# One round of weight conversion moves from unit 15 to unit 4, and four subtractions before the last layer move from VectorE to GpSimd

## The chip, the cores and the metric

The kernel runs on one core of a Trainium2 chip. The metric is the device time of one execution in microseconds; less is better. The engines are named as the profile names them: PE is TensorE's matmul, PEld its weight load, DVE is VectorE, ACT is ScalarE, POOL is GpSimd, SP is SyncE, which issues the DMAs here.

## The reference, cut to what matters

Windowed attention feeds a mixture of four experts, weighted per token, and that feeds an MLP with a gate. The MLP's weights arrive as float64.

```python
x = attention(q, k, v)                       # 1152 tokens x 512
p = domain_probs / (domain_probs.sum(-1, keepdims=True) + 1e-09)
out = np.zeros((N, D), dtype=np.float32)
for e in range(4):
    h = np.maximum(x @ w1[e], 0.0)           # 512 -> 1024
    out += p[:, e:e + 1] * (h @ w2[e])       # 1024 -> 512
h = out @ w_in                               # 512 -> 2048, w_in and w_out are float64
g = h * (1.0 / (1.0 + np.exp(-1.702 * h)))
return (g @ w_out).astype(np.float32)
```

## The kernel before, in words

Every fp32 matmul is done as three matmuls on an upper and a lower part of each operand: high x high, high x low, low x high. The upper part is a rounding copy made by ACT, the lower part a subtraction made by DVE or POOL.

After the attention and the first expert (up to 136.91 us) the work goes by **units** of 256 hidden columns. Units 4 to 15 are the experts 1 to 3 (the mixture); units 16 to 23 are the MLP. Tokens are split in two halves: c = 0 has 512 tokens as 2 x 256 columns, c = 1 has 640 as 2 x 320. The first layer of a unit and half, named ("1", s, c), is done by `first2` as seven block products instead of eight, into four PSUM banks in the order a, c, b, d, a, c, d. Each product is six matmuls (L798); the fourth product d uses the weight sums `wsh`/`wsl`, the last product adds to bank d again. Between the two uses of bank d, DVE must read it (`s`, L817, which is s + d). So the last product of a pass waits for that L817. The second layer of a unit and half is ("2", s, c), with accumulation by L912.

The order on PE is ("1", s, 0), ("2", s-1, 1), ("1", s, 1), ("2", s, 0) for each unit. After each product or output tile a **slot** is run: side work that is issued there by hand-written tables, `FIRST` for unit 4, `MID` for units 5 to 14, `TURN` from unit 15 to 18. A table's fields, divided by "|", are the slots in order. In a field, `p.s.i` are the steps of `w1_prep` for unit s (weight sums on POOL at L677, upper parts on ACT, lower parts `wal` L681 and `wsl` L685 on POOL unless `BY_VECTOR` names them), `q.s.i` those of `w2_prep` (`w2l`, L696), `l` weight loads, `d` a step of the gate or the shares that had been put off, and `c.c.m.i` the steps of `x2_turn`, which makes for the MLP the differences `xt` (L622) and the upper and lower parts of the mixture's output.

The side work of interest is the **conversion of float64 words to fp32**, 32 rounds in all. A round is taken up step by step by the letter `w`: a load of one round's words two rounds ahead, a (two ACT passes, L730 and L731, on the loaded tile `sd`), b (DVE, L736, reads `sd` and makes `m`), c (DVE, L740, and then POOL, L741, both on `m`), and the store of the round before. The tile `sd` has three buffers and `m` two. `x.0` and `x.1` are the first two loads.

Every engine runs its instructions in the order in which they are issued, so an instruction that waits holds up all behind it on its engine. SP's queue does the same for DMAs.

Of the kernel before, what the change touches and what calls it, by code (L numbers as in the profile page):

```python
# [13 lines left out]
ALU = mybir.AluOpType  # L14
# [95 lines left out]
def fused_kernel(ctx: ExitStack, tc: tile.TileContext, qk, v, dp, w1, w2, w_in, w_out, out):  # L110
# [17 lines left out]
    nc = tc.nc  # L128
# [457 lines left out]
    S0 = SM - 1  # L586
    HOLD = ((4, 1), (15, 0), (18, 0),)
    LOWER = {(0, 0): "ppp", (0, 1): "pvp", (1, 0): "pvv", (1, 1): "vvp"}
    TILES = (range(0, 4), range(4, 9))
    queue = []  # L590
    turn_ = [0]
# [11 lines left out]
    def combos(c, m, xf, t, whole, lo_engines=(nc.vector,) * 3):  # L603

        n, t0, q0 = N_[c], T0[c], Q0[c]
        th, tl = (late["t"][:, y, :, m, q0:q0 + n] for y in range(2))
        b = xf
        fns = []

        def lo_(eng, out_, whole_, hi_):  # L610
            eng.tensor_tensor(out=out_, in0=whole_, in1=hi_.bitcast(F32), op=ALU.subtract)

        def block(y, l):
            kt = 2 * (y // 2) + m
            cols = slice(t0 + l * n, t0 + (l + 1) * n)
            return [lambda: nc.scalar.activation(xh[:, kt, cols], b[y], AF.Copy),
                    lambda: lo_(nc.vector if c == 0 or y == 3 else lo_engines[0], xl[:, kt, cols], b[y], xh[:, kt, cols])]

        if whole:
            fns += block(0, 0)  # L620
        for y, (p, q_) in enumerate(((b[1], b[0]), (b[3], t[:, 0]), (b[3], b[1]), (b[2], t[:, 1]))):
            fns.append(lambda y=y, p=p, q_=q_: nc.vector.tensor_tensor(out=t[:, y], in0=p, in1=q_, op=ALU.subtract))  # L622
        for x, ys in enumerate((slice(0, 2), slice(2, 4))):
            fns.append(lambda ys=ys: nc.scalar.activation(th[:, ys, :], t[:, ys], AF.Copy))
            fns.append(lambda x=x, ys=ys: lo_(lo_engines[1 + x], tl[:, ys, :], t[:, ys], th[:, ys, :]))
        if whole:
            fns += block(2, 0) + block(3, 1)
        return fns
# [4 lines left out]
    def x1_combos(c, m, it):  # L633

        n, t0 = N_[c], T0[c]
        made = []

        def join():
            xf, t = big_pair(c, f"1_{c}{m}")
            for j in range(2):  # L640
                parts_ = [x.bitcast(F32)[:, 2 * j + m, t0:t0 + 2 * n].rearrange("p (l n) -> p l n", l=2) for x in (xh, xl)]
                nc.gpsimd.tensor_tensor(out=xf[:, 2 * j:2 * j + 2], in0=parts_[0], in1=parts_[1], op=ALU.add)
            made.extend(combos(c, m, [xf[:, y] for y in range(4)], t, False))

        def some(a_, b_):
            for fn in made[a_:b_]:
                fn()
        at_it(it, join)
        at_it(it + 1, lambda: some(0, 4))
        at_it(it + 2, lambda: some(4, 8))  # L650

    def x2_turn(c, m):

        n, t0 = N_[c], T0[c]
        pool = f"big{c}"
        t = late[pool].tile([P, 4, n], F32, tag=pool, name=f"xt2_{c}{m}")
        b = [final[c, h, 2 * j + m] for j in range(2) for h in range(2)]
        return combos(c, m, b, t, True, [{"p": nc.gpsimd, "v": nc.vector}[x] for x in LOWER[c, m]])


    BY_VECTOR = ("p.15.2", "p.15.3", "p.15.9", "p.16.0", "p.17.1", "p.17.2", "p.18.3", "p.18.5", "p.18.7", "q.16.1", "q.16.3", "q.17.3", "u.16.1", "u.17.1",)
    ENDS = {(15, 0): 1, (15, 1): 0, (17, 0): 0}

    def engine(name):
        return nc.vector if name in BY_VECTOR else nc.gpsimd

# [252 lines left out]
    def second2(s, c, slots):  # L919
        n = N_[c]  # L920
        h = hbuf2[s, c]
        wh, wl = wt[s, 1]
        for i, t in enumerate(TILES[c]):

            end = s == SE - 1 and c == 1 and i == len(TILES[c]) - 1
            for cols in (slice(0, DM // 2), slice(DM // 2, DM)) if end else (slice(0, DM),):
# [84 lines left out]
    def order_of(keys):  # L1011
        pe = [("1", keys[0])]
        for x in range(1, len(keys)):
# [10 lines left out]
    pe += order_of([(SM, 1), (SM + 1, 1)] + [(s, c) for s in range(SM + 2, SE) for c in range(2)])[1:]  # L1024

    TURN = {
# [18 lines left out]
    }  # L1045

    FIRST = {
# [3 lines left out]
    }  # L1051

    MID = {
# [49 lines left out]
    def due(kind, s, c):  # L1103

        one = 7 + len(TILES[1 - c])
        if kind == "1":
# [86 lines left out]
```

## Time and profile before

| what | value |
|---|---|
| median of 3 runs | 618.14 us (617.94 to 618.57) |
| profiled execution | 618.13 us |
| its span, first to last instruction | 616.4 us |
| PE busy in the span | 609.0 us (99%) |
| DVE, POOL, ACT busy | 477.1, 360.1, 273.0 us |
| granted TensorE clock | 1.00 throughout |

The profiled execution's 618.13 us is its span and 1.73 us around it. It lies 0.01 us from the median of the runs. A busy PE is not a PE at its peak, since the ends of matmuls are modelled: short waits are read from the distance of starts.

### The profile page before, as it was taken

The numbers are of one execution on the slowest core, as the hardware profiler recorded it, in microseconds if no ns is written. First come the engines' busy times: TensorE is split into PE (matmuls) and PEld (weight loads), VectorE is DVE, ScalarE is ACT, GpSimd is POOL, SyncE is SP. The second block draws the span as 40 slices with busy tenths as digits, with TensorE's granted clock in tenths as the row PEclk, the third lists the DMA queues.
The fourth block names the chain that finished last, engine by engine and source line by source line (L and its number), as shares of the span: only waits on it lengthen the run. The fifth ranks groups of instructions, "written<-read, shape, count | busy, mean of one in ns | idle before, by whom it ended". The sixth has DMA issues, their size and how long they took to land.

```text
span 616.4 us, 11216 instructions
## 1 busy us (share of the span) xinstructions
PE 609.0 (99%) x4153; PEld 569.9 (92%) x4153; DVE 477.1 (77%) x1006; ACT 273.0 (44%) x603; POOL 360.1 (58%) x340
## 2 busy tenths in 40 slices
PE   7999999999999999999999999999999999999997
PEld 5999999999999999999999999899898988998996
DVE  6987623968888888888888899999977667667565
ACT  7965111344434444444354453446555444444321
POOL 6564003675777877868669765767509473473310
PEclk9999999999999999999999999999999999999999
DMA  8874246013544555535456435022103121100004
GB/s 316 286 245 122 81 119 216 1 34 137 172 126 149 151 179 155 149 127 166 123 152 184 147 104 171 35 87 71 65 2 103 35 70 35 34 1 1 0 2 154
DMA packets 30502, 69.44 MB, mean 113 GB/s; under 512 B 6732, under 2 KB 11248, under 8 KB 30448
## 3 DMA queue, kind: packets, MB, share of 16 engines
q1 hardware_dynamic: 30448, 68.73, 35.4%
q8 instruction: 32, 0.52, 0.4%
q14 instruction: 22, 0.18, 0.1%
HBM read 55.99 MB, written 12.73 MB: 111 GB/s over the span
## 4 chain that ended last, share of the span: by engine, by line
PE 94%; DVE 3%; issue 1%; ACT 1%; POOL 1%; POOLq 0%; DVEq 0%; ACTq 0%
PE gd L798 10%; PE gc L798 10%; PE ga L798 9%; PE g L532 8%; PE q L902 8%; PE q L904 8%; PE q L903 8%; PE q L932 5%; PE q L930 5%; PE q L931 5%; PE gb L798 5%; PE pa L566 3%; PE pa L568 3%; PE pa L567 3%; DVE xt L622 0%
## 5 line engine op out<-in xcount | busy, mean ns | idle before, releaser
L902 PE MATMUL q<-h,w2h 128*128 128x320 f32 (+1 forms) x288 | 97.4, 338 | 0.1
L904 PE MATMUL q<-h,w2h 128*128 128x320 f32 (+1 forms) x288 | 97.2, 337 | 0.0
L903 PE MATMUL q<-h,w2l 128*128 128x320 f32 (+1 forms) x288 | 97.2, 337 | 0.0
L845 DVE TENSOR_TENSOR h<-cc,h 128x256 fp32r<-128x256 f32 (+1 forms) x80 | 73.9, 924 | 20.0 <-ACT h L835 12.5
L741 POOL TENSOR_TENSOR m<-m,sd 128x512 int32<-128x512 int32 x32 | 49.1, 1534 | 62.8 <-ACT h L835 36.8
L685 POOL TENSOR_TENSOR wsl<-ss,wsh 128x512 fp32r<-128x512 f32 x39 | 59.6, 1535 | 31.0 <-ACT wsh L684 20.6
L835 ACT ACTIVATE h<-cc 128x256 fp32r<-128x256 f32 (+3 forms) x48 | 32.9, 686 | 99.1 <-DVE cc L832 98.8
L912 DVE TENSOR_TENSOR acc<-q,acc 128x512 f32<-128x512 f32 (+1 forms) x132 | 69.9, 546 | 8.3 <-PE q L904 7.1
L820 POOL TENSOR_TENSOR cc<-s,u 128x256 f32<-128x256 f32 (+1 forms) x38 | 33.4, 878 | 59.9 <-DVE s L817 59.9
L904 PEld LDWEIGHTS q<-h,w2h 128*128 128x128 f32 x288 | 54.1, 188 | 4.4
L902 PEld LDWEIGHTS q<-h,w2h 128*128 128x128 f32 x288 | 54.1, 188 | 4.2 <-DVE acc L912 0.3
L903 PEld LDWEIGHTS q<-h,w2l 128*128 128x128 f32 x288 | 54.1, 188 | 3.9
L932 PE MATMUL q<-w2h,h 128*128 128x512 f32 (+1 forms) x146 | 56.9, 390 | 0.0
L930 PE MATMUL q<-w2h,h 128*128 128x512 f32 (+1 forms) x146 | 56.7, 389 | 0.0
L931 PE MATMUL q<-w2l,h 128*128 128x512 f32 (+1 forms) x146 | 56.5, 387 | 0.0
L696 POOL TENSOR_TENSOR w2l<-st,w2h 128x512 fp32r<-128x512 f32 x37 | 53.0, 1444 | 5.5 <-ACT w2h L695 5.2
L939 DVE SCALAR_TENSOR_TENSOR acc<-q,acc 128x512 f32<-128x512 f32 (+1 forms) x64 | 42.6, 677 | 11.7 <-PE q L932 11.3
L681 POOL TENSOR_TENSOR wal<-st,wah 128x512 fp32r<-128x512 f32 (+1 forms) x38 | 48.0, 1268 | 2.3 <-ACT wah L680 2.3
L798 PE MATMUL ga<-xh,wal 128*128 128x256 f32 (+1 forms) x160 | 47.3, 296 | 0.0
L798 PE MATMUL ga<-xl,wah 128*128 128x256 f32 (+1 forms) x160 | 47.3, 295 | 0.0
L798 PE MATMUL ga<-xh,wah 128*128 128x256 f32 (+1 forms) x160 | 47.2, 295 | 0.0
L832 DVE SCALAR_TENSOR_TENSOR cc<-cc,pb 128x256 f32<-128x256 f32 (+3 forms) x48 | 41.8, 871 | 1.0
(368 smaller groups left out, 1730.2 us busy)
## 6 DMA issues: line engine op xcount, KB each, us to landing
st<-in_w_dram SPq DMA_DIRECT2D x32, 512.0 KB, 5.0
sd<-in_w_in_dram SPq DMA_DIRECT2D x16, 512.0 KB, 4.1
sd<-in_w_out_dram SPq DMA_DIRECT2D x16, 512.0 KB, 4.0
w<-m SPq DMA_DIRECT2D x32, 256.0 KB, 4.4
st<-w SPq DMA_DIRECT2D x16, 512.0 KB, 3.5
out_dram<-acc SPq DMA_DIRECT2D x8, 256.0 KB, 2.0
pb<-pd SPq DMA_DIRECT2D x3, 320.0 KB, 3.5
pb<-pd SPq DMA_DIRECT2D x3, 256.0 KB, 4.5
```

The costliest lines, as they stand in the source:

```text
L532: nc.tensor.matmul(pt[:, :C], w[:, kt, fs], xx[:, kt, c * C:(c + 1) * C], start=first and y == 0, stop=not todo and y == len(products[x]) - 1)
L685: fns.append(lambda x=x, dst=dst: engine(f"p.{s}.{x}").tensor_tensor(out=sl[:, dst], in0=sums[:, dst], in1=sh[:, dst].bitcast(F32), op=ALU ...
L696: fns.append(lambda o=o: engine(f"q.{s}.{2 * o + 1}").tensor_tensor(out=lo[:, o], in0=t[:, o], in1=hi[:, o].bitcast(F32), op=ALU.subtract))
L798: nc.tensor.matmul(bank_[:, :n], wz[:, y, m, :], xz, start=start and m == 0 and z == 0, stop=m == 1 and z == 2, skip_group_check=not start)
L845: nc.vector.tensor_tensor(out=hl[:, sub], in0=cc[:, sub], in1=hh[:, sub].bitcast(F32), op=ALU.subtract)
L902: nc.tensor.matmul(pt, wh[:, o, cols], hi, start=first, stop=False, skip_group_check=both)
L903: nc.tensor.matmul(pt, wl[:, o, cols], hi, start=False, stop=False, skip_group_check=both)
L904: nc.tensor.matmul(pt, wh[:, o, cols], lo, start=False, stop=last, skip_group_check=both)
L912: nc.vector.tensor_tensor(out=dst[:, on], in0=pt[:, on], in1=src[:, on], op=ALU.add)
L930: nc.tensor.matmul(pt, hi, wh[:, o, cols], start=o == 0, stop=False)
L931: nc.tensor.matmul(pt, hi, wl[:, o, cols], start=False, stop=False)
L932: nc.tensor.matmul(pt, lo, wh[:, o, cols], start=False, stop=o == 1)
```

## The change

One round's worth of conversion steps leaves the slots of ("1", 15, 0), where five `w` stood, and joins unit 4, where nine `w` stand instead of four; the first two loads move forward. From then on every round comes one round earlier in its table than before, up to the end. At the turn from mixture to MLP, three differences (`xt`, 128x320) go from DVE to POOL, and so does one lower part (`w2l` of unit 17, 128x512); one ACT copy and what follows it moves by a slot.

```diff
+    BY_POOL = ((1, 0, 3), (1, 1, 0), (1, 1, 3))
...
-            fns.append(lambda y=y, p=p, q_=q_: nc.vector.tensor_tensor(out=t[:, y], in0=p, in1=q_, op=ALU.subtract))
+            eng = nc.gpsimd if whole and (c, m, y) in BY_POOL else nc.vector
+            fns.append(lambda y=y, p=p, q_=q_, eng=eng: eng.tensor_tensor(out=t[:, y], in0=p, in1=q_, op=ALU.subtract))
...
-    BY_VECTOR = (..., "q.16.1", "q.16.3", "q.17.3", "u.16.1", "u.17.1",)
+    BY_VECTOR = (..., "q.16.1", "q.16.3", "u.16.1", "u.17.1",)
...
-        ("1", 15, 0): " |  | w | w | w | w w | ",
+        ("1", 15, 0): " |  |  |  |  |  | ",
...
-        ("1", 16, 0): "q.17.1 c.1.0.12 | q.17.2 c.1.0.4 c.1.0.3 |  | c.1.0.10 c.1.0.5 | c.1.0.0 c.1.0.6 |  | q.16.3 c."
+        ("1", 16, 0): "q.17.1 c.1.0.12 | q.17.2 c.1.0.4 c.1.0.3 |  | c.1.0.10 | c.1.0.5 c.1.0.0 c.1.0.6 |  | q.16.3 c."
...
     FIRST = {
-        ("1", 0): "q.0 p.6 p.0 p.2 p.1 |  |  | p.3 q.2 l.0 |  | x.0 | p.4 | x.1",
-        ("1", 1): "p.8 d | p.7 q.1 | d w p.9 | w | d | p.10 w |  | p.5",
-        ("2", 0): "d |  |  | p.11 l.1 d w d q.3",
+        ("1", 0): "q.0 p.6 p.0 p.2 p.1 | x.0 |  | p.3 q.2 l.0 | x.1 |  | p.4 | ",
+        ("1", 1): "p.8 d w | p.7 q.1 | d w p.9 | w | d w | p.10 w | w | p.5 w",
+        ("2", 0): "d | w |  | p.11 l.1 d w d q.3",
```

In what follows rows of the changed kernel have line numbers that are 1 or 2 higher. A row is the line, the operation, output <- inputs with a running number, and the shape; the brackets say whose semaphores it waits on.

**DVE in ("1", 4, 1) and after it.** Before, from the sum u of that pass on:

```order
L815 TENSOR_TENSOR u_4_1_2056<-gb_1_2052,s_4_1_2054 128x320 [waits PE_49,Activation_49]
L817 TENSOR_TENSOR s_4_1_2057<-gd_1_2053,s_4_1_2055 128x320 [waits PE_49,Activation_49]
L845 TENSOR_TENSOR h_0_2026<-cc_0_1974,h_0_2026 128x768 [waits Activation_49]
L832 SCALAR_TENSOR_TENSOR cc_1_2058<-ga_1_2050,pb_1512_1952 128x320 [waits DMAHW2_49,PE_49]
L845 TENSOR_TENSOR h_1_2105<-cc_1_2058,h_1_2105 128x320 [waits Activation_49]
L736 TENSOR_SCALAR m_2116<-sd_2036 128x512 [waits DMAHW4_49]
```

With the change (its step b of round 0 is the row of m_2096, its step c the next one of m_2096):

```order
L817 TENSOR_TENSOR u_4_1_2056<-gb_1_2052,s_4_1_2054 128x320 [waits PE_49,Activation_49]
L738 TENSOR_SCALAR m_2096<-sd_2000 128x512 [waits DMAHW3_49,Activation_49]
L819 TENSOR_TENSOR s_4_1_2057<-gd_1_2053,s_4_1_2055 128x320 [waits PE_49]
L847 TENSOR_TENSOR h_0_2030<-cc_0_1974,h_0_2030 128x768 [waits DVE_49]
L742 SCALAR_TENSOR_TENSOR m_2096<-sd_2000,m_2096 128x512 [waits DVE_49]
L834 SCALAR_TENSOR_TENSOR cc_1_2058<-ga_1_2050,pb_1512_1952 128x320 [waits DMAHW2_49,PE_49]
L847 TENSOR_TENSOR h_1_2109<-cc_1_2058,h_1_2109 128x320 [waits Activation_49]
```

Step b of round 0 has moved up by four rows, in front of s, and it waits there for ACT; step c follows three rows later. Round 1 is new in unit 4: its step b stands ahead of the first L912 of ("2", 4, 0), its step c behind the second.

**POOL at the end of unit 4.** Before, from the sum cc of ("1", 4, 1) on; `wsl_1988` is the lower part of unit 5's weight sums:

```order
L820 TENSOR_TENSOR cc_1_2058<-s_4_1_2057,u_4_1_2056 128x320 [waits DVE_49]
L681 TENSOR_TENSOR wal_1986<-st_5_1603,wah_1985 128x512
L685 TENSOR_TENSOR wsl_1988<-ss_1984,wsh_1987 128x512 [waits Activation_49,Pool_49]
L741 TENSOR_TENSOR m_2116<-m_2116,sd_2036 128x512 [waits DMAHW0_49,DMAHW4_49,DVE_49,PE_49]
L696 TENSOR_TENSOR w2l_1982<-st_5_1605,w2h_1981 128x512
```

With the change:

```order
L822 TENSOR_TENSOR cc_1_2058<-s_4_1_2057,u_4_1_2056 128x320 [waits DVE_49]
L743 TENSOR_TENSOR m_2096<-m_2096,sd_2000 128x512 [waits DMAHW0_49,DVE_49,DMAHW3_49,PE_49,Activation_49]
L683 TENSOR_TENSOR wal_1986<-st_5_1603,wah_1985 128x512
L743 TENSOR_TENSOR m_2134<-m_2134,sd_2028 128x512 [waits DMAHW5_49,DVE_49,Activation_49]
L687 TENSOR_TENSOR wsl_1988<-ss_1984,wsh_1987 128x512 [waits Pool_49]
L698 TENSOR_TENSOR w2l_1982<-st_5_1605,w2h_1981 128x512
```

Two conversion steps now stand ahead of `wsl_1988`, and the second is step c of round 1.

**DVE at the turn, in ("1", 16, 0) and ("1", 17, 0).** With the change, from s of unit 16 to s of unit 17:

```order
L819 TENSOR_TENSOR s_16_0_5381<-gd_0_5377,s_16_0_5379 128x256 [waits PE_49,Activation_49]
L843 SCALAR_TENSOR_TENSOR cc_0_5382<-th_0_5428,ga_0_5374 128x256 [waits Activation_49]
L855 TENSOR_TENSOR cc_0_5382<-gc_0_5375,u_16_0_5380 128x256 [waits DVE_49,PE_49]
L847 TENSOR_TENSOR h_0_5427<-cc_0_5382,h_0_5427 128x256 [waits Activation_49]
L698 TENSOR_TENSOR w2l_5308<-st_16_4830,w2h_5307 128x512
L861 TENSOR_TENSOR cc_0_5382<-gd_0_5377,u_16_0_5380 128x256 [waits PE_49]
L612 TENSOR_TENSOR t<-xt_10_5364,t 128x2x320 [waits Activation_49]
L843 SCALAR_TENSOR_TENSOR cc_0_5382<-th_0_5428,cc_0_5382 128x768 [waits Activation_49]
L817 TENSOR_TENSOR u_17_0_5456<-gb_0_5452,s_17_0_5454 128x256 [waits PE_49,Activation_49]
L819 TENSOR_TENSOR s_17_0_5457<-gd_0_5453,s_17_0_5455 128x256 [waits PE_49,Activation_49]
```

Before, an `xt` stood ahead of the first row, a `w2l` behind the L612 row and an `xt` behind the second L843 row. These three now stand on POOL, between its sums cc of unit 16 and of unit 17; the fourth moved operation comes after the sum of unit 17.

## Rows read from the trace of the kernel before

**Rows 1.** The page: head, busy time of each engine, a DMA issue (last: us to landing).

```profile
span 616.4 us, 11216 instructions
...
PE 609.0 (99%) x4153; PEld 569.9 (92%) x4153; DVE 477.1 (77%) x1006; ACT 273.0 (44%) x603; POOL 360.1 (58%) x340
...
st<-in_w_dram SPq DMA_DIRECT2D x32, 512.0 KB, 5.0
```

**Rows 2.** Busy time of each engine in unit 4's stretch and at the turn.

```profile
core 0: us, PE busy (x) PEld busy (x) DVE busy (x) ACT busy (x) POOL busy (x), PEclk, DMA share, GB/s
136.91:153.69 16.78, 16.78 (x109) 15.71 (x109) 13.22 (x23) 7.18 (x14) 10.29 (x10) 1.00 0.35 126
422.60:434.65 12.05, 11.80 (x94) 11.48 (x94) 11.89 (x25) 7.84 (x18) 6.46 (x6) 1.00 0.39 119
```

**Rows 3.** Timeline of PE at its longest waits: start us, us, line, operation [idle before].

```profile
398.99 0.31 PE L798 MATMUL gc<-t,wsl 128*128 128x320 f32 x1
399.57 0.56 PE L798 MATMUL gb<-t,wsh 128*128 128x320 f32 x2 [0.27 <-DVE cc L853]
...
433.15 0.28 PE L798 MATMUL gc<-xh,wsl 128*128 128x256 f32 x1
433.68 0.50 PE L798 MATMUL gd<-t,wah 128*128 128x256 f32 x2 [0.25 <-DVE s L817]
```

**Rows 4.** Timeline of DVE in unit 15 and at the turn, same columns.

```profile
396.30 1.44 DVE L740 SCALAR_TENSOR_TENSOR m<-sd,m 128x512 uint32<-128x512 uint32 x1
...
433.22 0.41 DVE L817 TENSOR_TENSOR s<-gd,s 128x256 f32<-128x256 f32 x1
```

**Rows 5.** Timeline of ACT in ("1", 4, 1).

```profile
145.46 0.85 ACT L835 ACTIVATE h<-cc 128x768 fp32r<-128x768 f32 x1 [1.06 <-DVE cc L832]
...
146.77 0.67 ACT L731 ACTIVATE sd<-sd 128x512 f32<-128x512 f32 x1
```

**Rows 6.** Timeline of DVE in unit 4, and one row of unit 5.

```profile
145.35 0.48 DVE L815 TENSOR_TENSOR u<-gb,s 128x320 f32<-128x320 f32 x1
145.75 0.48 DVE L817 TENSOR_TENSOR s<-gd,s 128x320 f32<-128x320 f32 x1
146.34 1.66 DVE L845 TENSOR_TENSOR h<-cc,h 128x768 fp32r<-128x768 f32 x1
147.93 0.48 DVE L832 SCALAR_TENSOR_TENSOR cc<-ga,pb 128x320 f32<-128x320 f32 x1
148.94 0.57 DVE L845 TENSOR_TENSOR h<-cc,h 128x320 fp32r<-128x320 f32 x1 [0.54 <-ACT h L835]
149.43 0.41 DVE L736 TENSOR_SCALAR m<-sd 128x512 uint32<-128x512 uint32 x1
...
151.67 0.68 DVE L912 TENSOR_TENSOR acc<-q,acc 128x512 f32<-128x512 f32 x1
...
154.80 0.67 DVE L740 SCALAR_TENSOR_TENSOR m<-sd,m 128x512 uint32<-128x512 uint32 x1
...
178.65 1.36 DVE L845 TENSOR_TENSOR h<-cc,h 128x960 fp32r<-128x960 f32 x1
```

**Rows 7.** Timeline of PE: last product of ("1", 4, 1), wsl in ("1", 5, 0).

```profile
147.22 0.46 PE L798 MATMUL gd<-t,wah 128*128 128x320 f32 x2
...
156.08 0.28 PE L798 MATMUL gd<-t,wsl 128*128 128x256 f32 x1
```

**Rows 8.** Timeline of POOL in units 4 and 5, and at the turn.

```profile
149.57 1.43 POOL L685 TENSOR_TENSOR wsl<-ss,wsh 128x512 fp32r<-128x512 f32 x1 [0.41 <-ACT wsh L684]
155.60 2.11 POOL L741 TENSOR_TENSOR m<-m,sd 128x512 int32<-128x512 int32 x1 [4.61 <-DVE m L740]
...
177.66 1.33 POOL L741 TENSOR_TENSOR m<-m,sd 128x512 int32<-128x512 int32 x1 [3.35 <-ACT h L835]
178.95 1.67 POOL L681 TENSOR_TENSOR wal<-st,wah 128x256 fp32r<-128x256 f32 x1
...
433.71 1.39 POOL L820 TENSOR_TENSOR cc<-s,u 128x256 f32<-128x256 f32 x1 [4.81 <-DVE s L817]
```

More of the change, by code (lines that the diff above doesn't have):

```diff
@@ L658, in x2_turn @@
         return combos(c, m, b, t, True, [{"p": nc.gpsimd, "v": nc.vector}[x] for x in LOWER[c, m]])
-    BY_VECTOR = ("p.15.2", "p.15.3", "p.15.9", "p.16.0", "p.17.1", "p.17.2", "p.18.3", "p.18.5", "p.18.7", "q.16.1", "q.16.3", "q.17.3", "u.16.1", "u.17.1",)
+    BY_VECTOR = ("p.15.2", "p.15.3", "p.15.9", "p.16.0", "p.17.1", "p.17.2", "p.18.3", "p.18.5", "p.18.7", "q.16.1", "q.16.3", "u.16.1", "u.17.1",)
     ENDS = {(15, 0): 1, (15, 1): 0, (17, 0): 0}
```

## The prediction

> **What bounds the kernel now.** I read the page first: PE is busy for 609.0 of 616.4 us, DVE for 477.1, POOL for 360.1 [rows 1]. So the end is set by PE, and only what makes PE wait, or stop waiting, moves it. A table of busy times by stretch comes next. In unit 4's stretch PE has no gap (16.78 of 16.78 us), DVE is busy for 13.22 and POOL for 10.29; at the turn DVE is busy for 11.89 of 12.05 us and PE loses some time [rows 2]. The reader is to see that the round leaves a crowded place for one with room on average, and that an average says nothing about who stands in front of whom.
>
> Then the timeline of PE, by the distance of starts. A matmul of 320 columns follows the one before after 0.15 us (a row of two lasts 0.46, one lasts 0.31), one of 256 columns by its size after about 0.12. At 399.57 the distance is 0.58 and the pair after it takes 0.56 instead of 0.46: 0.58 - 0.15 + 0.10 = 0.53 us lost to DVE in unit 15. At 433.68 it is 0.53 - 0.12 + 0.10 = 0.51 us, again to DVE [rows 3]. A wait of under 0.2 us near 428 is left out of the sum. So some 1.0 to 1.2 us is all that the change can win in the places that it relieves.
>
> **What it takes away.** In unit 15 steps b and c of one round go from DVE, and step c alone took 1.44 us there; without them L853, for which PE waited, comes more than 0.53 us sooner, and I count the 0.53 us as won. At the turn PE waited for L817, which ended at 433.22 + 0.41 = 433.63 [rows 4]. Ahead of it DVE loses an `xt`, a `w2l` and another `xt`. Their sizes are those of L815 (0.48) and L912 (0.68), so this is some 1.4 us less DVE work. Whether it is won is taken up below.
>
> **What it adds in unit 4: step b of round 0.** Before, b stood behind h of 128x320 and waited for nothing. Now it stands between u and s of ("1", 4, 1). It reads what the second ACT pass of step a writes, and step a can't come sooner, since ACT starts the h ahead of it at 145.46, when DVE releases it, and then runs L730 and L731 up to 146.77 + 0.67 = 147.44 [rows 5]. DVE is done with u at 145.75 and now stands still until 147.48 (0.04 for the hand-over, an estimate). Step b takes 0.34 (149.43 to the next start, 149.77, the 0.41 of its row less the usual overlap). So s starts at 147.82 and not at 145.75, 2.07 us later, and ends at 148.30 [rows 6]. The last product of that pass may not write bank d before s has read it. PE wants to start it at 147.22 [rows 7] and starts at 148.35: a first stall of 1.13 us, and 0.1 for the start again.
>
> **What it adds in unit 4: round 1.** `wsl` of unit 5 (second half) was made by POOL at 149.57, long before its use. Now it stands behind two steps c on POOL, and the second waits for DVE, which does it only after two of the four L912 of ("2", 4, 0). I follow DVE from its late s, with the distances of the rows [rows 6]:
> - s 147.82, to h 0.59, to cc 1.59: 150.00.
> - Step c of round 0 is put in, 0.67 less an overlap of 0.07: 150.60.
> - cc to h of 128x320 takes 1.01: 151.61. From there to the first L912 took 151.67 - 148.94 = 2.73, with one step b in it, as now: 154.34. POOL's step c of round 0 runs from about 150.8 for 1.33 us, across that h, and can hold it for up to 0.5. I take 0.4: 154.74.
> - Of the 154.80 - 151.67 = 3.13 us to the old step c, two L912 (0.60 each) now come later: 1.93, so step c of round 1 starts at 156.67 and ends at 157.34.
>
> POOL's part starts 0.13 us after that (before: 155.60 after 154.80 + 0.67) and takes 1.33: 158.80. Two L912 after step c, DVE wants h of 128x960, at 156.67 + 0.60 + 1.20 = 158.47, and finds POOL busy. The rows show what happens then. At 178.65 such an h waited until POOL's L741 (177.66 + 1.33 = 178.99) ended. It ended itself at 180.01, so it ran for 1.02 us, and the POOL operation that had started at 178.95 took 1.67 us, twice what its 128x256 would by the 1.43 of 128x512. So the DVE operation with two inputs in SBUF goes first, and POOL's next one waits for it [rows 6, 8].
>
> The Trainium skill ("SBUF — State Buffer", the section on SBUF's two separate sides) has a rule for this: VectorE with two SBUF inputs and GpSimd share a port pair that one of them holds for a whole instruction while the other is blocked. The trace agrees in these rows. The rule speaks against the change, since work given to GpSimd blocks VectorE for longer than it took there; it names no winner where both wait.
>
> So h runs 158.80 to 159.82, and `wsl` after it for 1.28 (1.43 less 0.15, since that row met DVE too; an estimate): 161.1. PE wanted this matmul at 156.08 [rows 7]. Everything behind it is late by **161.1 - 156.1 = 5.0 us**, and the first stall is part of that, not added. Nothing gives it back: PE has no slack behind, and the other engines catch up while it stands. Bounds: without the hold of 0.4 and with `wsl` ahead of h it is 5.0 - 0.4 - 1.0 = 3.6; with the whole hold of 0.5 and a full 1.43 for `wsl` 5.25.
>
> Units 5 to 14 do the same steps in the same slots as before, only on the next round, so I count nothing there. The two loads that come first on SP, and the weight load that now stands behind one of them, cost nothing: a load lands 5.0 us after its issue [rows 1], and that weight load is for unit 6, whose sums begin behind unit 4's stretch, after 153.69 [rows 2]. The unit 14 that ends the rounds has steps b and c side by side, which puts one L859 behind by 0.6 us; its reader is DVE's next step, not PE, and it is hidden by the L912 that wait for PE there. If that cover were gone it would cost up to 0.6.
>
> **What the turn gives back.** POOL was idle for 4.81 us ahead of its sum at 433.71 [rows 8]. An `xt`, a `w2l` and an `xt` of 0.9, 1.3 and 0.9 us (by size from 1.43 for 128x512) now run there, 3.1 us. They fit, but beside them DVE has four operations with two SBUF inputs (h, `w2l` of unit 16, L611 and L841), and by the holding seen above each can stand behind one of POOL's. Also the copy for L611 waits for the `xt` that POOL now makes, 0.9 and not 0.48 us long. DVE saves 1.4 us and can lose up to 0.4 + 1.2 + 0.9. So of the 0.51 us at 433.68 between all and minus 0.9 is won; I take 0.1. With unit 15: 0.53 + 0.1 = 0.6 won, between 1.2 and minus 0.4.
>
> **Sum** against the profiled execution's own 618.13 us (0.01 from the median of 618.14): + 5.0 - 0.6 = 622.5 us. This is 0.7% slower.
>
> **The rivals.**
> 1. `wsl` gets ahead of h on the shared side, and the turn gives all it can: + 3.6 - 1.2, 620.5 us. For it: POOL's queue has the next operation ready at once. Against it: the row at 178.95.
> 2. Unit 4 hides the whole round: 618.13 - 1.1, about 617.0 us, faster. The mechanism is that ACT is done with step a before DVE reaches step b, and DVE with round 1 soon enough for `wsl` at 156.08. It decides where ACT's L731 ends by 145.7 and DVE's second step c by 156.08 - 1.28 - 1.33 - 0.13 = 153.3. For it: DVE is idle for 3.6 of 16.78 us there. Against it: L731 ended at 147.44 behind an h that DVE itself releases, and the L912 ahead of step c were not started before 151.67 in a program without these steps.
> 3. The turn gets worse, since POOL's three operations hold DVE at each step: + 5.2 + 0.4, 623.7 us. For it: DVE is busy 11.89 of 12.05 us there. Against it: POOL's 4.81 us of room.
> 4. The two effects cancel, within 0.2%: the stall in unit 4 would have to be under 2 us, that is `wsl` done by 158, before even step c of round 1 on POOL is (158.8).
>
> A stall of some 3.7 us at `wsl` is longer than any wait in the rows above; the granted clock is 1.00 in all of them [rows 2]. The Trainium skill ("TensorE: Matmul & The Clock Gate", the section on the clock gate) says that an idle PE can fall back to the lower of its two levels, and no run here shows it. If the rows of the changed kernel show 1.2 GHz after the stall, each us of work at that level costs another us.
>
> **How the numbers follow.** The forecast's own mechanism with middle values 0.55, rival 1 0.15, rival 3 with or without a lower clock 0.17, rival 2 0.07, rival 4 0.06. A change of 0.2%, 1.2 us, is about what a measurement of this kernel can tell from none. Slower by more than that: 0.55 + 0.15 + 0.17 = 0.87; within it 0.06; faster 0.07. The range takes in rivals 1 and 3 with a few tenths to spare: 619.8 to 624.3.
>
> **What the profile after would show.** Right: in ("1", 4, 1) DVE's step b follows u after a wait for ACT, and the last product of that pass starts some 1.1 us late. Step c of round 1 starts on DVE at 156 to 157, `wsl` of unit 5 ends on POOL at about 161, and PE's wait of 3 to 4 us in ("1", 5, 0) names POOL's `wsl`. From there to unit 14 each unit takes as long as before. The wait at 399 is gone, that at 433 is not. Wrong: no PE wait in units 4 and 5 (ACT or DVE was earlier than I think), or `wsl` ahead of step c on POOL in time, or waits that go on through units 5 and 6 because POOL does not catch up.

## The result, and the profile after

The changed kernel takes **627.84 us** (median of 5 runs, 626.34 to 628.97) against 618.57 us of the kernel before on the same chip (617.94 to 618.79): a measured ratio of 1.0139, 95% interval 1.0120 to 1.0159 (the quotient of the two medians alone is 1.0150). The forecast was 622.5 us in a range of 619.8 to 624.3. The direction was right, the size was not: slower by 9.3 us where 4.4 were forecast.

The head of its page and its busy times, which answer to [rows 1]:

```profile
span 624.6 us, 11214 instructions
...
PE 612.1 (98%) x4153; PEld 572.2 (92%) x4153; DVE 475.4 (76%) x1002; ACT 273.1 (44%) x603; POOL 363.9 (58%) x344
```

The span grew by 8.2 us, PE's busy time by 3.1. DVE does four instructions less and POOL four more, and both are busy for about as long as before: an average shows nothing of what happened. PE's list of waits does (what was waited for, us in total, times, the longest):

```profile
PE gd L800 <- POOL wsl L687: 3.2, 1, 3.2
PE gd L800 <- DVE s L819: 1.3, 2, 0.9
...
PE q L932 <- ACT h L844: 0.4, 1, 0.4
PE q L934 <- DVE h L847: 0.3, 1, 0.3
```

To see where each falls I took the start of the same matmul in both traces and followed the difference. It is 0.30 us ahead of the change's first effect (other runs of these kernels show minus 0.1 to 0.7 there), and then:

| place | difference after it, us | gained or lost by it |
|---|---|---|
| last product of ("1", 4, 1) | 1.40 | 1.1 lost |
| `wsl` in ("1", 5, 0) | 5.00 | 3.6 lost |
| the rest of that pass and the next, up to 172 us, with no wait listed | 6.50 | 1.5 lost |
| units 6 to 14, to 380 us | 6.16 | flat, back by 0.3 in two small steps |
| unit 15, first half | 6.27 | 0.1 lost: a new wait of 0.5, the old one gone |
| ahead of the turn | 6.10 | |
| turn, up to the second product into bank a of ("1", 17, 0) | 7.45 | 1.35 lost |
| behind the old wait of [rows 3] at 433.68 | 6.97 | 0.5 won |
| second layer of the MLP's first unit | 8.25 | 1.3 lost |

**Units 4 and 5.** DVE and POOL in the timeline, which answer to [rows 6, 8]:

```profile
147.74 0.43 DVE L738 TENSOR_SCALAR m<-sd 128x512 uint32<-128x512 uint32 x1 [1.61 <-ACT sd L733]
148.08 0.48 DVE L819 TENSOR_TENSOR s<-gd,s 128x320 f32<-128x320 f32 x1
148.48 0.95 DVE L847 TENSOR_TENSOR h<-cc,h 128x768 fp32r<-128x768 f32 x1
149.34 1.37 DVE L742 SCALAR_TENSOR_TENSOR m<-sd,m 128x512 uint32<-128x512 uint32 x1
...
156.68 0.68 DVE L742 SCALAR_TENSOR_TENSOR m<-sd,m 128x512 uint32<-128x512 uint32 x1
...
158.47 1.33 DVE L847 TENSOR_TENSOR h<-cc,h 128x960 fp32r<-128x960 f32 x1
```

```profile
157.49 1.30 POOL L743 TENSOR_TENSOR m<-m,sd 128x512 int32<-128x512 int32 x1 [3.75 <-ACT h L837]
158.74 2.19 POOL L687 TENSOR_TENSOR wsl<-ss,wsh 128x512 fp32r<-128x512 f32 x1
```

Step b stands still for 1.61 us until ACT has made `sd`, and s goes with it. Step c of round 1 comes at 156.68 on DVE, its other half on POOL up to 158.79. The h that wants to run at 158.47 stays until 159.80: it waits for POOL and then runs. `wsl`, in its turn behind that h, takes 2.19 instead of 1.43 us and ends at 160.93. PE, which answers to [rows 7]:

```profile
148.62 0.56 PE L800 MATMUL gd<-t,wah 128*128 128x320 f32 x2 [0.93 <-DVE s L819]
...
160.98 0.39 PE L800 MATMUL gd<-t,wsl 128*128 128x256 f32 x1 [3.24 <-POOL wsl L687]
...
162.40 0.34 PE L800 MATMUL gc<-xl,wsh 128*128 128x256 f32 x1
162.54 0.42 PE L800 MATMUL gc<-xh,wsl 128*128 128x256 f32 x1
162.75 0.42 PE L800 MATMUL gc<-xh,wsh 128*128 128x256 f32 x1
```

The starts are 0.12 us apart up to 162.40, then 0.14, then 0.21. No releaser stands behind these rows. The table by stretch says why (columns as in [rows 2]; the granted clock is the third number from the end):

```profile
162.50:165.70 3.20, 3.20 (x16) 3.20 (x15) 2.62 (x6) 0.77 (x2) 2.81 (x4) 0.50 0.95 267
165.70:168.90 3.20, 3.20 (x23) 3.20 (x22) 2.21 (x5) 1.39 (x3) 0.49 (x1) 0.97 0.21 77
```

The clock is at the lower of its two levels, 1.2 GHz, through these 3.2 us, after PE had stood for 3.24 and then worked for 1.4. k1_words, whose edit is given below, shows the same in its own trace: a wait of 3.2 us for `wsl`, and 1.5 us lost behind it. A PE that is slowed by its clock counts as busy, which is where about half of PE's 3.1 us more of busy time comes from.

**Unit 15.** The wait of [rows 3] at 399 is gone, and another has come in the pass ahead of it. DVE's h and POOL's `w2l` there, first before (a row that ends in x2 holds two operations):

```profile
393.74 1.42 DVE L845 TENSOR_TENSOR h<-cc,h 128x960 fp32r<-128x960 f32 x1
...
395.73 3.17 POOL L696 TENSOR_TENSOR w2l<-st,w2h 128x512 fp32r<-128x512 f32 x2
```

With the change, and PE's new wait:

```profile
400.42 2.23 DVE L847 TENSOR_TENSOR h<-cc,h 128x960 fp32r<-128x960 f32 x1
```

```profile
400.33 3.44 POOL L698 TENSOR_TENSOR w2l<-st,w2h 128x512 fp32r<-128x512 f32 x2 [1.03 <-ACT w2h L697]
```

```profile
403.36 0.50 PE L800 MATMUL gd<-t,wah 128*128 128x256 f32 x2 [0.38 <-DVE s L819]
```

POOL's first `w2l` starts 0.09 us ahead of the h, so the h stands behind it until it ends, and s is late. Before, `w2l` came behind the h. What turned them round is the end of unit 14, where steps b and c of the last round now stand side by side on DVE: POOL's half of c runs at 396.71, 2.3 us sooner against PE than before (6.16 us taken off, against 392.84). DVE's L834 beside it takes 1.21 us where it took 0.81, the h starts 0.5 us later against PE (400.42 less 6.16, against 393.74), and POOL, done with all ahead of it, starts `w2l` as soon as ACT's `w2h` is there.

**The turn.** Two of DVE's rows before, at the place where the second layer's inputs are made:

```profile
433.55 0.94 DVE L845 TENSOR_TENSOR h<-cc,h 128x768 fp32r<-128x768 f32 x1
...
436.27 0.41 DVE L845 TENSOR_TENSOR h<-cc,h 128x256 fp32r<-128x256 f32 x1
```

With the change, POOL, DVE and PE from ("1", 16, 0) on, which answer to [rows 3, 4, 8]:

```profile
434.79 0.88 POOL L624 TENSOR_TENSOR xt<-acc,xt 128x320 f32<-128x320 f32 x1
435.63 1.48 POOL L698 TENSOR_TENSOR w2l<-st,w2h 128x512 fp32r<-128x512 f32 x1
437.07 1.31 POOL L624 TENSOR_TENSOR xt<-acc 128x320 f32<-128x320 f32 x1
440.74 0.74 POOL L822 TENSOR_TENSOR cc<-s,u 128x256 f32<-128x256 f32 x1 [2.36 <-DVE s L819]
...
443.90 0.88 POOL L624 TENSOR_TENSOR xt<-acc,xt 128x320 f32<-128x320 f32 x1 [0.86 <-DVE xt L624]
```

```profile
435.33 0.62 DVE L847 TENSOR_TENSOR h<-cc,h 128x256 fp32r<-128x256 f32 x1
435.88 1.78 DVE L698 TENSOR_TENSOR w2l<-st,w2h 128x512 fp32r<-128x512 f32 x1
...
440.84 1.45 DVE L847 TENSOR_TENSOR h<-cc,h 128x768 fp32r<-128x768 f32 x1 [0.25 <-ACT h L844]
...
444.07 0.99 DVE L847 TENSOR_TENSOR h<-cc,h 128x256 fp32r<-128x256 f32 x1
```

```profile
438.05 0.50 PE L800 MATMUL gd<-t,wsh 128*128 128x256 f32 x2 [0.68 <-DVE cc L861]
439.20 0.39 PE L800 MATMUL ga<-xh,wah 128*128 128x256 f32 x1 [0.17 <-ACT s L811]
448.26 0.50 PE L932 MATMUL q<-w2h,h 128*128 128x512 f32 x1 [0.42 <-ACT h L844]
```

The three moved operations run back to back on POOL, from 434.79 to 438.38. DVE's own `w2l` stands behind POOL's and takes 1.78 us. L861 of unit 16 is queued behind it, and unit 17's first product into bank d may not start until L861 has read that bank. The h of 128x256 takes 0.99 us beside the fourth moved operation (443.90), and 0.62 where POOL's `xt` ends early enough (435.33); before it took 0.41. The h of 128x768 ahead of it starts 0.10 us behind POOL's sum (440.74) and takes 1.45. Before it started 0.16 ahead of that sum, took 0.94, and the sum was the one that took long (433.71, 1.39 us, [rows 8]). The h of 128x256 is followed by L861, ACT's tanh, L843, ACT's h and DVE's h, and PE waits at the end of that chain, in the second layer.

### The profile page after: what moved, and what is told of

The parts are those of the page before. It is cut to its first block, busy times and chain, and to the rows that moved or that the text cites. A ratio compares the mean times of both kernels' runs of the same rounds, so it can differ in the third digit from the quotient of the medians.

```text
span 624.6 us, 11214 instructions
## 1 busy us (share of the span) xinstructions
PE 612.1 (98%) x4153; PEld 572.2 (92%) x4153; DVE 475.4 (76%) x1002; ACT 273.1 (44%) x603; POOL 363.9 (58%) x344
## 4 chain that ended last, share of the span: by engine, by line
PE 92%; DVE 4%; ACT 1%; issue 1%; DMA 0%; POOL 0%; DVEq 0%; ACTq 0%
PE gd L800 10%; PE ga L800 9%; PE gc L800 9%; PE g L532 8%; PE q L904 8%; PE q L906 8%; PE q L905 8%; PE q L934 5%; PE q L932 5%; PE q L933 5%; PE gb L800 5%; PE pa L566 3%; PE pa L568 3%; PE pa L567 3%; DVE h L847 1%
## 5 line engine op out<-in xcount | busy, mean ns | idle before, releaser
L847 DVE TENSOR_TENSOR h<-cc,h 128x256 fp32r<-128x256 f32 (+1 forms) x80 | 75.2, 940 | 19.9 <-ACT h L837 12.4
L698 POOL TENSOR_TENSOR w2l<-st,w2h 128x512 fp32r<-128x512 f32 x38 | 56.4, 1498 | 6.8 <-ACT w2h L697 6.5
L683 POOL TENSOR_TENSOR wal<-st,wah 128x512 fp32r<-128x512 f32 (+1 forms) x38 | 45.4, 1199 | 2.3 <-ACT wah L682 2.3
L834 DVE SCALAR_TENSOR_TENSOR cc<-cc,pb 128x256 f32<-128x256 f32 (+3 forms) x48 | 42.6, 886 | 1.0
```

Of the source, the lines that this page charges most:

```text
L698: fns.append(lambda o=o: engine(f"q.{s}.{2 * o + 1}").tensor_tensor(out=lo[:, o], in0=t[:, o], in1=hi[:, o].bitcast(F32), op=ALU.subtract))
L847: nc.vector.tensor_tensor(out=hl[:, sub], in0=cc[:, sub], in1=hh[:, sub].bitcast(F32), op=ALU.subtract)
```

## The experiments

Ten kernels were run, each with five rounds against the kernel before. The first four shared one chip (before: 618.48 us), the next four another (618.35), the last two a third (618.66). Every ratio but that of k10_c15 is clear of 1, that of k7_w2l only just.

| kernel | what it is | median, us | ratio to before, 95% |
|---|---|---|---|
| k1_words | the round's move alone | 624.35 | 1.0104 (1.0090 to 1.0119) |
| k2_pool | the four POOL operations alone | 620.40 | 1.0033 (1.0021 to 1.0045) |
| k3_wsl | the change, step c of round 1 behind `wsl` | 623.19 | 1.0085 (1.0071 to 1.0098) |
| k4_both | k3_wsl, step b of round 0 behind s | 622.03 | 1.0057 (1.0045 to 1.0069) |
| k5_spin | the change, PE kept at work in the wait | 624.82 | 1.0117 (1.0100 to 1.0133) |
| k6_xt | the three `xt` alone on POOL | 619.96 | 1.0029 (1.0018 to 1.0041) |
| k7_w2l | `w2l` of unit 17 alone on POOL | 619.01 | 1.0009 (1.0001 to 1.0018) |
| k8_all | k1_words with three places mended | 620.21 | 1.0030 (1.0018 to 1.0041) |
| k9_turn | k2_pool, DVE's `w2l` behind L861 | 620.47 | 1.0026 (1.0016 to 1.0036) |
| k10_c15 | before, unit 15's step c later | 618.79 | 1.0001 (0.9992 to 1.0009) |

### The two halves apart: k1_words and k2_pool

k1_words is the diff without its `BY_POOL`, `BY_VECTOR` and ("1", 16, 0) parts, k2_pool is those parts alone.

> Only the move of the conversion round; the turn is as before. Place theory (the loss is made of three separate things: two waits behind moved rows in units 4 and 5, 5.0 us together; PE's lower clock after the second, 1.5 us in the profile and more in some runs; POOL's operations at the turn, 1.8 us): before + 5.0 + 1.5 to 3, less nothing at unit 15, so 624 to 626.5 us, with a clock of 0.5 after the wait for wsl. Load theory (DVE and POOL have too much to do, wherever it stands): the same unit 4, but also a loss in the units behind it; the starts of the passes then drift on after 172 us.

> Only the four operations at the turn go to POOL; the round stays in unit 15. Place theory: units 4 to 15 as before, and between 420 and 450 us PE waits for L861 behind a w2l that POOL's w2l holds, for ACT's s, and for h: before + 1.5 to 2.2, 620.1 to 620.8 us. Rival (the turn's loss comes from arriving there some 6 us late or from unit 15's changed order, not from POOL's operations): within 0.5 us of before.

The times are those of the place theory in both. The round's move costs 5.9 us and the four operations 1.9, by the medians. In k1_words the start of the same matmul is 6.1 us late at 172 us and 6.0 at the end: units 6 to 23 add nothing. In k2_pool nothing is late ahead of the turn, and 2.1 us are lost in it. So by the starts the two parts add up to the whole and hardly touch each other. The medians add up to 7.8 us of the 9.3; the median run of the changed kernel has a lower mean clock than that of k1_words (0.995 against 0.997).

### The clock: k5_spin

```diff
         nc.vector.tensor_tensor(out=u2, in0=b[:, :n], in1=s1, op=ALU.add)
+        if (s, c) == (NF + 1, 0):
+            for _ in range(15):
+                nc.tensor.matmul(d[:, :512], idle[:, :P], idle[:, :512], start=True, stop=True)
         product(d, S_, 2, 2, None, True)
```

> The changed kernel with 15 matmuls of 512 columns on constants ahead of the product that waits for wsl in (1,5,0), into the bank that this product then starts anew; the result is untouched. wsl comes as late as before, so PE only has something to do meanwhile. Clock theory (the fall to half level comes from PE standing still there): the clock stays at 1.00, the last two products of that pass keep 0.12 us a matmul, and the time falls by the 1.5 us that the profile showed, or by more where runs lost more: 624.5 to 625.5 us, with the runs within 1 us of each other. Rival (the fall has another cause, as the load of the chip at that moment): no change from 627.8 us and a spread of over 2 us.

The wait for `wsl` is as long as before, and PE does idle work in it, on constants, into a bank that it overwrites. Its table by stretch and three rows of its timeline of PE:

```profile
155.00:161.50 6.50, 6.44 (x40) 4.52 (x40) 5.26 (x8) 2.67 (x5) 3.88 (x3) 1.00 0.60 187
161.50:166.00 4.50, 4.50 (x36) 4.50 (x36) 3.48 (x8) 0.93 (x2) 3.95 (x5) 1.00 0.96 297
```

```profile
161.10 0.39 PE L800 MATMUL gd<-t,wsl 128*128 128x256 f32 x1
...
162.63 0.28 PE L800 MATMUL gc<-xh,wsl 128*128 128x256 f32 x1
162.75 0.28 PE L800 MATMUL gc<-xh,wsh 128*128 128x256 f32 x1
```

`wsl` comes 0.12 us later than in the changed kernel, but the granted clock stays at 1.00 and the starts stay 0.12 us apart: behind the wait, up to 172 us, 0.1 us is lost against the kernel before, not 1.5. The profiled run is 1.4 us shorter (625.08 against 626.47). The median is 3.0 shorter, but the two were measured apart and the intervals of their ratios overlap, so the size of the gain rests on the traces. So the 1.5 us behind the wait were the clock, and PE's standing still was its cause. The Trainium skill ("TensorE: Matmul & The Clock Gate", the section on the clock gate) has an idle PE fall back to its lower level; these rows agree (0.50 behind the wait of 3.24 us, 1.00 with PE at work in it).

The scatter goes with the clock. The changed kernel's five runs show a mean clock of 0.997, 0.996, 0.995, 0.995 and 0.992, and take 626.34, 626.47, 627.84, 627.84 and 628.97 us. k5_spin has four runs at 0.999 or 1.00 with 624.75 to 625.08 us, and one at 0.994 with 627.74, so the spread of under 1 us that the clock theory expected did not come. All ten runs of the two kernels that have the whole wait, the changed one and k1_words, are at 0.997 or below. But a low mean clock comes without it too: k3_wsl has one run of six at 0.995 (625.83 us), and the kernel before has two at 0.994 (621.16 and 620.87 us) of the 51 runs beside the ten kernels. So the wait makes the clock fall, and it is not the only thing that does; what did it in those runs, and how long the low level lasted in runs that have no trace, was not seen.

### The place in the queue: k3_wsl, k4_both and k8_all

k3_wsl puts step c of round 1 behind `wsl` (`p.11`) in ("2", 4, 0). k4_both moves step b of round 0 behind s as well. k8_all makes both shifts in k1_words and gives ("1", 5, 0) a table of its own, `FIVE`, in which ACT's step a of the next round stands behind ACT's copies s. Here are k4_both's lines, and behind the dots k8_all's table (the line that looks it up is left out):

```diff
-        ("1", 1): "p.8 d w | p.7 q.1 | d w p.9 | w | d w | p.10 w | w | p.5 w",
-        ("2", 0): "d | w |  | p.11 l.1 d w d q.3",
+        ("1", 1): "p.8 d w | p.7 q.1 | d w p.9 |  | d w w | p.10 w | w | p.5 w",
+        ("2", 0): "d |  |  | p.11 w l.1 d w d q.3",
...
+    FIVE = "w |  | p.0 w |  | w p.2 | p.1 | p.8 | "
```

> The changed kernel with step c of round 1 behind wsl instead of in front of it. Place theory: the wait for wsl in (1,5,0) and the low clock after it are gone, the wait of 1.2 us for s in (1,4,1) and the turn's loss stay: 618.6 + 1.2 + 2.0, about 621.8 us, clock 1.00. Load theory: the DVE work that was late before wsl is still late; a wait of 2 us or more turns up elsewhere in units 5 and 6, 624 us or more.

> As the one before, and step b of round 0 behind s instead of in front of it. Place theory: no wait in units 4 and 5, clock 1.00, the turn's loss stays: 620 to 621 us, 1.2 us below the kernel with wsl alone put right. Load theory: a wait of more than 1 us stays in units 4 to 6.

> The round's move alone (the turn as before) with three places put right: step b of round 0 behind s, step c of round 1 behind wsl, and step a of the round after them behind ACT's copies of banks a and c in (1,5,0), where a wait of 1.1 us had turned up. Place theory: no wait is left in units 4 and 5, and the time is that of before, 618.2 to 619 us. Load theory (DVE is too late there whatever the order): a wait of over 0.6 us turns up once more in unit 5, 619.2 us or more.

Each shift took away the wait that it was made for, but the waits did not end. In k3_wsl the 3.2 us for `wsl` and the low clock behind it are gone (clock 1.00 in the trace), and 1.1 us for ACT's s in ("1", 5, 0) is new. In k4_both the wait of ("1", 4, 1) is gone too, which is worth the 1.2 us that were expected, and ACT's s still costs 1.0 by PE's list of waits. So the place theory was too low for k3_wsl (623.2 us where 621.8 were expected) and for k4_both (622.0 where at most 621 were), and in k8_all the load theory came true (620.2 us). ACT's timeline in k4_both:

```profile
155.51 1.00 ACT L837 ACTIVATE h<-cc 128x960 fp32r<-128x960 f32 x1 [3.65 <-DVE cc L834]
156.43 0.65 ACT L732 ACTIVATE sd<-sd 128x512 int32<-128x512 uint32 x1
156.98 0.65 ACT L733 ACTIVATE sd<-sd 128x512 f32<-128x512 f32 x1
157.53 0.36 ACT L811 ACTIVATE s<-ga 128x256 f32<-128x256 f32 x1
```

Step a stands ahead of s on ACT, and both behind an h that waits for DVE. With step a out of the way (k8_all) PE waits for DVE itself: PE's row, DVE's rows, and DVE in the table by stretch (the third busy time):

```profile
160.08 0.51 PE L798 MATMUL gd<-t,wah 128*128 128x256 f32 x2 [1.12 <-DVE s L817]
```

```profile
153.45 1.11 DVE L736 TENSOR_SCALAR m<-sd 128x512 uint32<-128x512 uint32 x1
...
159.62 0.41 DVE L817 TENSOR_TENSOR s<-gd,s 128x256 f32<-128x256 f32 x1
```

```profile
153.69:161.20 7.51, 6.39 (x49) 5.97 (x47) 7.44 (x12) 2.69 (x5) 3.36 (x3) 1.00 0.37 124
```

DVE is busy for 7.44 of 7.51 us there, and without a gap up to PE's start at 160.08. So s comes sooner only if something that stands ahead of it goes behind it, or takes less time: step b at 153.45 takes 1.11 us where it took 0.41 in [rows 6], with POOL's `wsl` (152.74 to 154.28) beside it. Of k1_words' 5.9 us the three shifts took back 4.0 (of which 1.5 is the clock, by the start of the same matmul in its trace), and 1.9 stayed, 1.3 of them at this wait. Step c of round 1 (0.68 us at 157.61) still stands ahead of s. An order with step c behind s, or a round spread over a longer stretch with some of its steps in unit 5, was not tried.

### The four operations at the turn: k6_xt, k7_w2l and k9_turn

k6_xt leaves `w2l` of unit 17 on DVE, k7_w2l leaves the three `xt` there (`BY_POOL = ()`). k9_turn takes all four and issues DVE's `w2l` of unit 16 (`q.16.3`) one slot later, behind L861:

```diff
-        ("1", 16, 0): "q.17.1 c.1.0.12 | q.17.2 c.1.0.4 c.1.0.3 |  | c.1.0.10 | c.1.0.5 c.1.0.0 c.1.0.6 |  | q.16.3 c."
+        ("1", 16, 0): "q.17.1 c.1.0.12 | q.17.2 c.1.0.4 c.1.0.3 |  | c.1.0.10 | c.1.0.5 c.1.0.0 c.1.0.6 |  | c."
...
-        ("1", 17, 0): "c.1.0.9 | q.17.3 | c.1.1.10 c.1.1.2 |  | c.1.1.4 c.1.0.11 c.1.1.0 c.1.0.13 | c.1.1.3 c.1.1.6 | ",
+        ("1", 17, 0): "q.16.3 c.1.0.9 | q.17.3 | c.1.1.10 c.1.1.2 |  | c.1.1.4 c.1.0.11 c.1.1.0 c.1.0.13 | c.1.1.3 c.1.1.6 | ",
```

> The kernel before with the three differences alone on POOL; w2l of unit 17 stays on DVE. If POOL's w2l, which holds DVE's w2l of unit 16, is what costs at 437 us: that wait for L861 is gone and at most the later waits for h (near 447 us) stay, 618 to 619.2 us. If each POOL operation holds DVE alike: some three quarters of the loss stay, 620 us.

> The kernel before with w2l of unit 17 alone on POOL; the three differences stay on DVE. If this w2l is what costs: PE waits for L861 near 431 us (in the time of before) as with all four, 619.5 to 620.5 us. If each POOL operation holds DVE alike: a quarter of the loss, 619 us.

> The four GpSimd operations alone (620.4 us in k2_pool) with one more shift: DVE's w2l of unit 16, which POOL's xt and w2l stretch to 1.78 us, is issued behind L861 of unit 16 instead of ahead of it. Place theory: PE's first new wait at the turn (0.6 us for L861, since unit 17 writes the same bank d) and the wait for ACT's s behind it (0.2) vanish, the waits for h in the second layer (0.7) stay: 619.4 to 619.8. Load theory: the held w2l only moves in front of L612 and L843, h comes as late as before or later, and the waits grow there by what vanished: 620.1 to 620.7.

By the medians the three `xt` cost 1.6 us without the `w2l`, and the `w2l` 0.7 without them, against 1.9 together; both times are those expected if each POOL operation holds DVE alike. The starts of the same matmuls say more. The turn loses 2.0 us with the three `xt` alone, 0.7 with the `w2l` alone and 2.1 with all four, so the parts don't add up. Ahead of the second layer each kind loses 0.7 alone, since each holds one of DVE's operations ahead of L861: `w2l` of unit 16 takes 1.36 us in k6_xt, h 1.22 in k7_w2l, against 0.68 and 0.42 before. The 1.3 us in the second layer come with the `xt` and not with the `w2l`. So neither kind is harmless, and the `xt` cost more. k9_turn was to win the first wait of 0.6 us by place; it costs 1.8 us over before where k2_pool costs 1.9, which is no difference, and is what its load theory expected. DVE's rows:

```profile
429.47 0.41 DVE L861 TENSOR_TENSOR cc<-gd,u 128x256 f32<-128x256 f32 x1
429.81 1.45 DVE L698 TENSOR_TENSOR w2l<-st,w2h 128x512 fp32r<-128x512 f32 x1
431.19 1.49 DVE L612 TENSOR_TENSOR t<-xt,t 128x640 fp32r<-128x640 f32 x1
```

L861 is in time now and the wait for it is gone. The held `w2l` and L612 stand ahead of s instead, and PE's list of waits has 1.1 us for that s.

### Unit 15 without moving the round: k10_c15

```diff
-        ("1", 15, 0): " |  | w | w | w | w w | ",
+        ("1", 15, 0): " |  | w | w |  |  | w w w",
```

> The kernel before with one shift in unit 15, no round moved: step c (L740, 1.44 us there) is issued behind L853 and its L832 of the first half instead of ahead of the first L832. If step c in front of L853 is what PE waits for at 399, as the prediction said, that 0.53 us is won, and s of the second half comes at most 0.1 us too late for PE: 617.8 to 618.1 against 618.4, and the round need not leave unit 15 at all. If POOL's two w2l are what holds DVE there, or if s of the next pass is now late by as much, nothing is won: 618.3 to 618.7.

The time is that of the kernel before. DVE's L853 comes sooner and PE's wait at 399 shrinks by 0.4 us. But the h of 128x256 ahead of L853 stands behind POOL's `w2l` now (1.55 us, before 0.62), and L859 and s behind the moved step c. Two waits of 0.3 us come instead (waits, and DVE's timeline):

```profile
PE gd L798 <- DVE cc L859: 0.3, 1, 0.3
...
PE gd L798 <- DVE s L817: 0.3, 1, 0.3
```

```profile
397.37 1.55 DVE L845 TENSOR_TENSOR h<-cc,h 128x256 fp32r<-128x256 f32 x1 [0.48 <-ACT h L835]
...
399.72 0.68 DVE L740 SCALAR_TENSOR_TENSOR m<-sd,m 128x512 uint32<-128x512 uint32 x1
```

No version that beats the kernel before was found.

## Why the prediction was right about the sign and wrong about the size

- **The first stall in ("1", 4, 1): right.** Step b waits for ACT and s goes with it. The product was forecast for 148.35 and starts at 148.62, of which 0.30 is from ahead of unit 4. k1_words and k3_wsl show the same stall (1.1 us from the start of the same matmul), and k4_both, with b behind s, has none.
- **`wsl` behind step c and h: right, and nearer than its parts deserve.** Step c of round 1 was forecast for 156.67 and came at 156.68, h for 158.80 to 159.82 and was done at 159.80, the matmul of `wsl` for 161.1 and came at 160.98. The difference to before is 5.0 us with the 0.3 from ahead of it and 4.7 without, so agreement to hundredths is luck. One part was wrong as well: the forecast took the h of 128x768 and step c of round 0 with their old lengths, but h, no longer held, takes 0.95 us instead of 1.66, and step c, now beside POOL's sum, 1.37 instead of 0.67. The two errors of 0.7 us cancel. DVE goes first when POOL's operation ends, as read from [rows 6, 8], and rival 1 (620.5) is out by that.
- **The clock: named, but left without a price. This step failed.** The text said that each us of work at the lower level costs another us, gave a chance to a lower clock within rival 3, and put nothing into the sum or the range for it. It cost 1.5 us in the profiled run by PE's starts, and k5_spin, which takes the clock's fall away and leaves the wait, is 1.4 us shorter in its profiled run. The range needed an upper end that paid for it whenever the wait was as long as the sum itself said.
- **Unit 15: the 0.53 us at 399 are gone as counted, and lost again. This step failed, by 0.6 us.** The step "without them L853 comes more than 0.53 us sooner, and I count the 0.53 us as won" asked only what stands ahead of L853. The steps b and c side by side in unit 14 were seen, and called "hidden by the L912 that wait for PE there". They were not: they bring POOL's step c forward and DVE's h of 128x960 back, `w2l` gets ahead of that h, and the h takes 2.23 us. Net 0.1 us lost. The rows show the mechanism. The wait, 0.5 to 0.6 us by the starts, comes in all six kernels that move the round and in none of the other five; no run takes it away alone. k10_c15 shows that the place of step c is not what makes unit 15 short of time.
- **The turn: this step failed, by 2.2 us.** "DVE saves 1.4 us and can lose up to 0.4 + 1.2 + 0.9. So of the 0.51 us at 433.68 between all and minus 0.9 is won; I take 0.1." The losses were there: `w2l` at 1.78 us is 1.1 over the 0.68 of an operation of its size. And the 0.51 us at 433.68 were won. But the step followed one deadline alone, s of unit 17. L861 of unit 16 has an earlier one (bank d, 0.68 us), and h of unit 17 a later one (0.4 + 0.3 us at the second layer). The fourth operation, at 443.90, was said to come after the stretch and was not priced, and nor was the h of 128x768 that takes 1.45 us at 440.84, 0.10 us behind the start of POOL's own sum. k2_pool shows the loss apart from all else (1.0033), k6_xt that the three `xt` alone lose about as much (2.0 us by the starts), k7_w2l that `w2l` alone loses 0.7, k9_turn that with `w2l` behind L861 the loss moves to s and stays. Most of it is holding, by the rows. In k2_pool L861 of unit 16 comes 1.45 us late against PE, and the h and `w2l` ahead of it are 1.3 longer than before. From s to L861 of unit 17 it takes 1.4 us more, and the two h in between are 1.1 longer. What POOL's longer time for the same subtraction (0.88 against 0.48 us) adds, by ACT's copy that waits for it, was not separated.
- **Units 6 to 14 add nothing: right.** The difference is flat from 172 us to the end of unit 14; what the new order at that end does is the wait in unit 15 above.

**By terms, in the profiled run:** 0.3 ahead of unit 4, 4.7 for the two waits (forecast 5.0), 1.5 for the clock (0), minus 0.4 from unit 6 up to the turn (minus 0.53; unit 15 itself gave plus 0.1, and small waits elsewhere that are gone gave the rest), 2.1 at the turn (minus 0.1): 8.2 us, the difference of the spans. So against the forecast the turn is out by 2.2 us and the clock by 1.5, and that the errors in the smaller terms cancel is luck. The median lies another 1.4 us above the profiled run; a lower mean clock in those runs is all that is known of it. Rival 3 named the turn with the right mechanism, and with a price of 0.4 us that was a fifth of what it cost.

What the experiments add to the forecast's picture of unit 4: the three better orders that were tried do not hide the round there either. Rival 2 asked whether ACT and DVE come soon enough for two given readers. k8_all takes both of those waits away, and DVE, busy without a gap up to the next reader, makes PE wait there. That no order at all would hide it is not shown.

## What to carry to other kernels

Where the engine beside PE is busy for nearly all of a stretch, a wait that is mended by order can come back at the next reader, as it did in k3_wsl, k8_all and k9_turn; sum that engine's work up to each reader in turn, not up to the one at which PE waits today. A subtraction that went from VectorE to GpSimd left VectorE's queue but not its time here, since VectorE had two-input operations on SBUF beside it: list those with their readers before counting the saving. And a wait of some microseconds on TensorE is to be priced with the slower work that may come behind it, 1.5 us here behind 3.24.

## What the runs showed of the hardware that was not expected

- The clock did not fall in the wait but behind it: in the changed kernel PE stood for 3.24 us up to 160.98, worked at the full level to 162.40, and then at 0.50 in the stretch from 162.50 to 165.70. In k5_spin it stayed at 1.00 with fifteen idle matmuls in the same wait.
- Which engine is held can hang on a tenth of a microsecond or less. POOL's `w2l` that started 0.09 us ahead of DVE's h (400.33 against 400.42) held it until its own end, so that the h took 2.23 us. Where both wait, DVE goes first, and POOL's row is the long one (`wsl` 2.19 us at 158.74). The Trainium skill ("SBUF — State Buffer", the section on SBUF's two separate sides) says that one of the two holds the shared ports for a whole instruction, and these rows agree; that DVE wins the hand-over is from the rows alone.
